# Seven block products from group 2 on, two of them accumulated in PSUM: an attention and feed-forward kernel

## The chip, the cores and the metric

One core of one Trainium2 chip. The metric is the device time of one execution in microseconds; lower is better. Runs shown of the kernel before: 213.74, 213.37 and 212.76, median 213.37.

## The reference

Windowed attention with a linear distance bias and a few global keys, then a feed-forward layer with a softplus.

```
q, k, v: 4 sequences x 8 heads x 768 tokens x 64, float32;  8 global keys, window 96
scores = q k^T / 8 - slope[h] * dist        # dist: |i - j| in the window, 96 at a global key outside it
scores = -1e9 where a key is neither global nor in the causal window of 96
x = softmax(scores) v                       # 3072 tokens x 512
g = softplus(x @ w_in)                      # w_in 512 x 2048
out = g @ w_out                             # w_out 2048 x 512, result float32
```

## The kernel before

**Tiling.** The 3072 tokens are 24 blocks of 128. Two neighbouring blocks of a sequence are a unit (12 units), whose q, k and v are loaded together, 512 KB each. Two blocks are also a group of the feed-forward part (12 groups of 256 tokens). Matmuls are in bfloat16, sums in float32 PSUM.

**Attention of block n.** q and k are cast to bfloat16 (`cast_q`, L622; `cast_rows`, L641), transposed to put the head dimension on partitions (for units 0 to 2 on PE, `transp_pe`; from unit 3 on by a DMA transpose on SP's queue, `transp_dma`, L737), and multiplied for the block itself and the block before it (`scores`, L814). DVE adds the bias (z, L872), ACT takes the exponential (pb, L879), PE multiplies by v with a column of ones (`pv`, L885), DVE normalises (L909, L910), and the result is transposed into XT (`x_transp`, L919: on PE for blocks 0 to 5, by a DMA transpose on SP after that). The keys and values of the first GH rows are copied into the earlier block's buffers for the global keys (`globals_k`, `globals_v`, names gk and gv).

**Feed-forward of group g.** `mm1` (L947) makes the 2048 hidden features in 8 pieces a{g}.{p} of 8 matmuls each (128 x 256 columns), alternating two PSUM banks. ACT takes Exp of each piece (e, L971) and Ln(1 + e) of two pieces together (ln, L982), which gives the softplus g. The second layer has two forms:

- Groups 0 to 2: `mm2` (L996), for each of the two blocks 16 matmuls of 512 columns into one PSUM bank (b{g}.{ns}.{x}), then one copy out (oc, L1032) and a store.
- Groups 3 to 11: seven block products in place of eight (`products`, L456). The group's g is split in four quarters by block (2) and by half of the hidden features (2); w_out is split in four by half of the hidden features and half of the columns. `weight_sums` (L391) forms five sums of w_out's quarters once (ws, 20 operations); `token_sums` (L433) forms five differences of g's quarters for each group (ka, L447). Each product is 8 matmuls of 256 columns, b{g}.3, 4, 5, 2, 1, 7, 6 in this order, and all of groups 3 to 9 go through the one bank o_ps: its lower half takes 3, 5, 7 and 1, its upper half 4, 2 and 6. Groups 10 and 11 spread theirs over several banks (`S_KEYS`). The products are combined in osb, the output buffer, by the operations oe{g}:

| operation | engine | what it does |
|---|---|---|
| a (L498) | ACT or DVE | copies products 3 and 4 to the two off-diagonal quarters |
| b (L477, L478) | DVE | diagonal quarters = off-diagonal ones less 5 and less 2, two operations of 256 columns |
| c (L481) | DVE | off-diagonal quarters + 5 and 2 |
| 1 (L495) | DVE | both diagonal quarters + product 1 |
| 7 (L490) | DVE | diagonal quarters + 7 and 6 (one operation when these lie in one bank, two of L485 when not) |

A product can be written to a half of o_ps only when the operation that reads the earlier product there is done.

**Buffers and loads.** Every load goes to one of 12 raw buffers of 4 KB per partition (NRAW, L307). q, k and v give theirs back; the 8 loads of w_out keep theirs (with 2 spare ones, which hold weight sums), and from the weight sums on three of the 8 return. So 5 rotate later on. The order of the first loads is `FIRST_LOADS` (L152). How far ahead of its block a later unit is loaded is set by `LEADS` (L154) in groups, through a wait on an mm1 piece. Nearly all loads, stores and DMA transposes are issued by SP, whose queue is in order: one that waits holds all behind it.

**Order.** The instruction order of all engines is one written list, `ORDER` (L68): each name with its engine (P PE, V DVE, A ACT, G POOL, S SP). Each engine takes its operations in that order; what an operation waits for follows from the data. 35 filler matmuls (L1116) stand between PE's first operations. The distances for the biases have buffers of their own (rel, far, dist, dist0, L329 to L332).

Of the kernel before, what the change touches and what calls it, by code (L numbers as in the profile page):

```python
# [68 lines left out]
blank:V ldq0.0:A iota:G ldk0.1:S fill0:P ldq0.1:A ldk0.0:S fill1:P dl1a:V fill2:P dl1c:V table:A ldq1.1:S dl0a:V  # L69
fill3:P dl0b:V ldv0:S fill4:P dl0c:V ldk1.0:S dl1e:V fill5:P d0:G fill6:P ldq1.0:S biasTrue6:A d0e:V biasTrue2:A  # L70
fill7:P biasFalse7:V biasFalse0:A biasFalse4:G fill8:P biasFalse3:A ldk1.1:S biasFalse1:A castq0.0:A fill9:P
castk0.1:G ldv1:S biasTrue4:A ident:G biasFalse2:A biasTrue7:A castq0.1:V win1:S biasTrue5:A castk0.0:A biasFalse6:V
trq0.0:P biasTrue1:V biasTrue0:A biasFalse5:V trk0.0:P biasTrue3:V cpq0.0:V fill10:P sb0.0:P cpk0.0:A cpq0.1:V
fill11:P cpk0.1:A castv0.00:G fill12:P fill13:P castq1.1:V ones:G castk1.0:A sc0.0:P sb1.0:P castv0.01:G ex0.0:A
sb1.1:P castq1.0:V ex0.1:A castv0.11:G sc1.0:P sc1.1:P ldq2.0:S ex1.0:A pv0.0:P fill14:P castk1.1:G win0:S nm0.0:V
ex1.1:A ldq2.1:S castv0.10:G trq1.0:P fill15:P ldk2.0:S pv0.1:P cpq1.0:A pv1.1:P nm0.1:V trk1.0:P ldk2.1:S cpq1.1:A
fill16:P nm1.1:V cin1:G pv1.0:P win2:S cpk1.1:A fill17:P xt0:P win3:S nm1.0:V cpk1.0:A fill18:P fill19:P win4:S
castv1.11:G castv1.01:A fill20:P castv1.00:V sc2.0:P win5:S castq2.0:G xt1:P cin0:A win7:S fill21:P z2.0:V fill22:P
fill23:P fill24:P win6:S gv4.1:G z2.1:V sc3.0:P castv1.10:A fill25:P gk4:G wout0:S xc1:V xc0:A fill26:P castq2.1:G
sc3.1:P z3.0:V ex2.0:A a0.1:P castk2.1:G ex2.1:A castk2.0:G pv2.0:P a0.0:P nm2.0:V wout7:S trq2.0:P z3.1:V e0.0:A  # L80
pv2.1:P cin2:G fill27:P ex3.0:A nm2.1:V trk2.0:P ex3.1:A cpq2.0:V fill28:P cin3:G xt2:P fill29:P fill30:P xc2:V
fill31:P e0.1:A fill32:P wout1:S pv3.0:P cin4:G ln0.0:A fill33:P wout2:S a0.3:P nm3.0:V ldv2:S cpk2.0:A a0.2:P
cin5:V e0.3:A cpk2.1:V pv3.1:P wout4:S a0.5:P e0.2:A cpq2.1:V cin7:G wout3:S ln0.1:A a0.4:P nm3.1:V e0.5:A sc4.0:P
cin6:V e0.4:A xt3:P ln0.2:A a0.7:P wout6:S z4.1:V cout0:G a0.6:P e0.7:A xc3:V gv4.0:G z4.0:V fill34:P a1.1:P e0.6:A
ldq3:S wout5:S ex4.1:A cout7:V a1.0:P gk8:V gk5:A cout1:V b0.0.0:P e1.0:A sc5.0:P ws0.6:V e1.1:A b0.0.2:P cout2:G
z5.0:V a1.2:P ln1.0:A a1.3:P ex4.0:A ws0.4:V b0.0.4:P castv2.10:V e1.3:A sc5.1:P castv2.00:V castv2.01:A b1.0.0:P
cout4:G z5.1:V b1.0.2:P e1.2:A pv4.0:P ln1.1:A a1.5:P castv2.11:G nm4.0:V cout3:G b0.1.0:P ln0.3:A ldk3:S pv4.1:P
b0.1.2:P nm4.1:V gv5.0:G gv5.1:A b1.0.4:P e1.5:A a1.4:P ws0.3:V ex5.1:A ws0.1:V b1.0.6:P b0.1.4:P cout6:V castq3.0:A
b0.1.6:P ws1.7:V xt4:P b0.1.8:P ex5.0:A xc4:V a1.7:P ws1.1:V e1.4:A b0.0.6:P ws1.4:V cout5:A ldv4:S pv5.0:P b0.0.8:P
trq3:S nm5.0:V castk3.00:G a1.6:P castk3.01:A ws1.6:V castk3.10:A pv5.1:P castk3.11:A b0.0.10:P nm5.1:V b0.0.12:P  # L90
gk6:A ln1.2:A trk3:S b0.1.10:P ws2.1:V b0.1.12:P ws0.7:V e1.6:A xt5:P b0.1.14:P e1.7:A ws1.3:V ws2.3:G b0.0.14:P
ln1.3:A b1.0.8:P xc5:V ldv3:S ws2.7:V b1.0.10:P castv4.11:A a2.0:P ws2.4:G a2.1:P oc0.0.0:V e2.0:A oc0.1.0:A
b1.0.12:P ws2.6:V e2.1:A b1.0.14:P gv6.0:G ldk4:S sc6.0:P oc1.0.0:A ldq4:S a2.2:P ln2.0:A z6.1:V st0.0.0:S ws3.7:G
ldq5:S a2.3:P e2.2:A z6.0:V ex6.1:A castv3.00:G b1.1.0:P a2.4:P castv3.10:G gk7:A castv3.01:V e2.3:A sc7.0:P e2.4:A
b1.1.2:P ex6.0:A z7.0:V b1.1.4:P castk4.00:G a2.5:P ln2.1:A gv6.1:G castk4.01:V b1.1.6:P castv3.11:G e2.5:A b1.1.8:P
castq4.0:V pv6.0:P ex7.0:A castk4.10:G b1.1.10:P ldk5:S b1.1.12:P nm6.0:V ln2.2:A trq4:S a2.7:P z7.1:V castk4.11:G
b1.1.14:P castv4.00:G pv6.1:P trk4:S a2.6:P oc1.1.0:A nm6.1:V gv7.0:G ex7.1:A b2.0.0:P gv7.1:V xt6:S ws3.3:V e2.7:A
pv7.0:P b2.0.4:P e2.6:A castk5.00:G nm7.0:V ln2.3:A castv4.10:G ldv5:S b2.0.8:P castv4.01:V castk5.10:G gv8.0:A
pv7.1:P b2.0.12:P nm7.1:V ws3.6:G sc8.0:P xt7:S oc2.0.0:A castq5.0:A gv8.1:G z8.1:V b2.1.0:P ws3.4:G st0.1.0:S
castk5.01:A b2.1.4:P trq5:S z8.0:V ex8.1:A b2.1.8:P castk5.11:G gk9:A castv5.10:V castv5.00:G ex8.0:A st1.1.0:S  # L100
sc9.0:P trk5:S a3.0:P castv5.01:G z9.0:V pv8.0:P a3.1:P e3.0:A ldq6:S nm8.0:V st1.0.0:S ex9.0:A z9.1:V pv8.1:P
a3.2:P e3.1:A gv9.0:G ln3.0:A nm8.1:V gv9.1:G ldk6:S ws3.1:G xt8:S pv9.0:P ex9.1:A a3.3:P nm9.0:V gk10:A e3.2:A
pv9.1:P sc10.0:P e3.3:A nm9.1:V a3.4:P castq6.0:G ln3.1:A z10.0:V xt9:S a3.5:P gv10.1:G e3.4:A gv10.0:V ex10.0:A
trq6:S a3.6:P z10.1:V e3.5:A b2.1.12:P castk6.11:G e3.6:A ldq7:S pv10.0:P ex10.1:A ldv6:S castk6.10:G a3.7:P
nm10.0:V ln3.2:A a4.0:P castk6.01:V gk11:G oc2.1.0:V e3.7:A sc11.0:P castk6.00:V ln3.3:A pv10.1:P trk6:S a4.1:P
z11.0:V gv11.1:G gv11.0:A b3.3:P castv5.11:G e4.1:A nm10.1:V st2.0.0:S e4.0:A b3.4:P st2.1.0:S ka3.6:V ldk7:S
ex11.0:A ka3.7:V xt10:S a4.2:P ka3.5:V oe3.a:A a4.3:P castv6.11:G castv6.00:A ka3.2:V ldv7:S e4.2:A ka3.1:G b3.5:P
e4.3:A z11.1:V ln4.0:A pv11.0:P b3.2:P nm11.0:V ex11.1:A a4.4:P oe3.b:V castq7.0:G a4.5:P e4.4:A oe3.c:V pv11.1:P
castv6.01:G sc12.0:P e4.5:A nm11.1:V b3.1:P castk7.00:G ln4.2:A z12.0:V xt11:S a4.6:P z12.1:V ex12.0:A a4.7:P
oe3.1:V ex12.1:A trq7:S castv7.00:G castk7.01:V sc13.0:P e4.7:A castv6.10:G pv12.0:P b3.7:P e4.6:A nm12.0:V ln4.1:A  # L110
castk7.11:G b3.6:P z13.0:V castk7.10:G ln4.3:A a5.1:P castv7.01:G oe3.7:V trk7:S pv12.1:P a5.0:P ka4.7:V e5.1:A
nm12.1:V ex13.0:A b4.3:P ldq8:S ka4.6:V e5.0:A a5.3:P z13.1:V pv13.0:P b4.4:P e5.3:A nm13.0:V ex13.1:A a5.2:P
ka4.5:V oe4.a:A gk14:V a5.5:P ka4.2:V e5.2:A ldk8:S xt12:S pv13.1:P b4.5:P e5.5:A nm13.1:V ln5.0:A b4.2:P ka4.1:V
xt13:S castq8.0:V ln5.1:A a5.4:P oe4.b:V st3.0.0:S sc14.0:P e5.4:A ldv8:S oe4.c:V a5.7:P trq8:S ln5.2:A castk8.01:G
z14.1:V castk8.00:G a5.6:P e5.7:A castv7.11:G z14.0:V b4.1:P ex14.1:A castv7.10:G a6.1:P castk8.10:G gk15:A e5.6:A
oe4.1:V castk8.11:G ex14.0:A sc15.0:P gv14.1:V gv14.0:G trk8:S a6.0:P ln5.3:A z15.0:V b4.7:P e6.1:A ka5.6:G
# [131 lines left out]
def kernel(  # L248
# [440 lines left out]
    def kt_unit(i):  # L689
        return kT_t(i)[:]  # L690
# [581 lines left out]
```

## Time and profile before

The profiled execution:

| | |
|---|---|
| its own time | 213.29 us |
| span from first to last instruction | 211.4 us |
| granted TensorE clock | 1.000 |
| busy us: PE / DVE / ACT / POOL | 202.0 / 161.0 / 179.3 / 106.9 |
| mm1 matmuls (L956) | 768, 94.5 us busy |
| block products (L512) | 504 |
| mm2 matmuls (L1003) | 96 |
| DMA | 40.98 MB, mean 194 GB/s |

Engines: PE is TensorE's matmuls, PEld its weight loads, DVE VectorE, ACT ScalarE, POOL GpSimd, SP SyncE (SPq: the issue of DMAs). Rows of the chain of waits are: start, length, engine and line. Rows of a group are: line, engine, operation, tiles and shapes, count; busy us and mean ns of one; idle time of the engine before them and what ended it. A stretch row is: from and to in us, length, then the busy us of PE, PEld, DVE, ACT and POOL (with counts), granted clock, DMA's busy share, GB/s. Matmul ends are modelled, so the distance between starts tells more of PE than a matmul's own duration. Some matmul records can be missing.

### The profile page before, as it was taken

How to read it: one execution, taken by the hardware profiler on the slowest of the kernel's cores; microseconds unless marked ns; L12 is line 12 of the kernel's file. 1: busy time of each engine (PE TensorE's matmuls, PEld its weight loads, DVE VectorE, ACT ScalarE, POOL GpSimd, SP SyncE). 2: the span in 40 equal slices, each digit the busy share in tenths (PEclk: the TensorE clock that was granted, in tenths of full speed). 3: DMA queues.
4: the chain of work that ended last, by engine and by line, in shares of the span. 5: the costliest groups of instructions: out<-in, count | busy, mean ns of one | idle time of the engine just before them, and what ended most of it. 6: DMA issues, size and time to landing. Idle time of an engine off the chain costs nothing.

```text
span 211.4 us, 5443 instructions
## 1 busy us (share of the span) xinstructions
PE 202.0 (96%) x2176; PEld 161.8 (77%) x2187; DVE 161.0 (76%) x292; ACT 179.3 (85%) x260; POOL 106.9 (51%) x130
## 2 busy tenths in 40 slices
PE   7987999999999988999999999999999999999994
PEld 2564786666765766988988889889889889988883
DVE  4665888888779976988798898786868989624554
ACT  6886999999998899888899989998999899877510
POOL 4466541618769463565038794564465436061070
PEclk9999999999999999999999999999999999999999
DMA  5999999949996899976399988777595510300413
GB/s 202 348 329 321 395 387 353 333 119 211 290 225 154 206 256 177 323 187 126 103 232 185 242 213 175 175 181 174 134 210 130 179 22 3 101 3 0 152 77 122
DMA packets 69848, 40.98 MB, mean 194 GB/s; under 512 B 30144, under 2 KB 61376, under 8 KB 69824
## 3 DMA queue, kind: packets, MB, share of 16 engines
q1 hardware_dynamic: 69392, 39.99, 71.4%
q10 hardware_dynamic: 432, 0.66, 0.9%
q8 instruction: 17, 0.28, 0.6%
q14 instruction: 7, 0.06, 0.1%
HBM read 27.26 MB, written 6.29 MB: 159 GB/s over the span
## 4 chain that ended last, share of the span: by engine, by line
PE 64%; ACT 14%; DMA 11%; SPq 3%; issue 3%; POOL 2%; DVE 2%; DVEq 0%; POOLq 0%
PE h_ps L956 29%; PE o_ps L512 22%; DMA raw<-in_moe_w_out_dram 5%; ACT e L971 4%; PE s_ps L846 4%; DMA raw<-in_moe_w_in_dram 4%; PE x_ps L898 3%; PE o_ps L1003 3%; ACT g L982 3%; ACT pb L879 3%; DMA raw<-in_q_dram 3%; SPq L573 2%; PE x_ps L512 2%; POOL w_out_bf L616 1%; PE s_ps L512 1%
## 5 line engine op out<-in xcount | busy, mean ns | idle before, releaser
L956 PE MATMUL h_ps<-XT,w_in_bf 128*128 128x256 bf16 x768 | 94.5, 273 | 2.4 <-ACT XT L934 1.4
L956 PEld LDWEIGHTS <-w_in_bf 128*128 128x128 bf16 x768 | 72.9, 98 | 13.5 <-issue 1.2
L971 ACT ACTIVATE e<-h_ps 128x512 f32<-128x512 f32 x96 | 58.3, 635 | 11.4 <-PE h_ps L956 11.1
L982 ACT ACTIVATE g<-e 128x1024 bf16<-128x1024 f32 x48 | 49.8, 1056 | 0.8
L872 DVE TENSOR_TENSOR z<-s_ps,biasA 128x1024 f32<-128x1024 f32 x38 | 45.8, 1218 | 4.7 <-PE s_ps L846 2.6
L879 ACT ACTIVATE pb<-z 128x1024 bf16<-128x1024 f32 (+1 forms) x44 | 43.2, 993 | 0.2
L512 PEld LDWEIGHTS <-g 128*128 128x128 bf16 x288 | 27.6, 98 | 3.2
L658 POOL CAST kb<-raw 64x512 bf16<-64x512 f32 x25 | 17.1, 682 | 23.6 <-DMA raw<-in_k_dram 11.0
L447 POOL TENSOR_TENSOR g<-g 128x1024 bf16<-128x1024 bf16 x7 | 15.3, 2187 | 19.3 <-DVE raw L447 17.2
L658 POOL CAST vb<-raw 64x512 bf16<-64x512 f32 x30 | 19.2, 641 | 7.2 <-DMA raw<-in_v_dram 5.8
L512 PEld LDWEIGHTS <-raw 128*128 128x128 bf16 x216 | 20.7, 98 | 2.5
L764 POOL COPY vb<-vb 4x512 bf16<-4x512 bf16 x19 | 12.1, 638 | 19.0 <-PE x_ps L898 18.6
L512 PE MATMUL o_ps<-raw,raw 128*128 128x256 bf16 x168 | 20.8, 273 | 0.0
L898 PEld LDWEIGHTS <-pb 128*128 128x128 bf16 x352 | 16.6, 97 | 4.9 <-ACT pb L879 0.9
L447 DVE TENSOR_TENSOR raw<-g 128x1024 bf16<-128x1024 bf16 x21 | 15.1, 729 | 4.5 <-PE s_ps L512 2.4
L910 DVE TENSOR_TENSOR xs<-x_ps,rcp 128x256 bf16<-128x256 f32 x40 | 17.0, 425 | 1.4
L512 PE MATMUL o_ps<-raw,g 128*128 128x256 bf16 x144 | 18.0, 273 | 0.0
L447 POOL TENSOR_TENSOR raw<-g 128x1024 bf16<-128x1024 bf16 x6 | 13.1, 2184 | 7.8 <-ACT g L982 7.6
L898 PE MATMUL x_ps<-vb,pb 128*128 128x65 bf16 x304 | 15.9, 193 | 0.6 <-DVE xs L910 0.4
L1003 PE MATMUL o_ps<-w_out_bf,g 128*128 128x512 bf16 x59 | 15.4, 379 | 0.4 <-DVE vb L658 0.2
L909 DVE RECIPROCAL rcp<-x_ps 128x4 f32<-128x4 f32 x40 | 7.2, 180 | 10.6 <-PE x_ps L898 10.1
L1003 PEld LDWEIGHTS <-g 128*128 128x128 bf16 x96 | 8.6, 98 | 6.7 <-ACT g L982 0.3
(110 smaller groups left out, 247.4 us busy)
## 6 DMA issues: line engine op xcount, KB each, us to landing
raw<-in_v_dram SPq DMA_DIRECT2D x12, 512.0 KB, 4.8
out_dram<-osb SPq DMA_DIRECT2D x22, 256.0 KB, 2.9
raw<-in_q_dram SPq DMA_DIRECT2D x9, 512.0 KB, 4.3
raw<-in_k_dram SPq DMA_DIRECT2D x9, 512.0 KB, 4.6
raw<-in_moe_w_in_dram SPq DMA_DIRECT2D x8, 512.0 KB, 8.1
raw<-in_moe_w_out_dram SPq DMA_DIRECT2D x8, 512.0 KB, 9.8
raw<-in_k_dram SPq DMA_DIRECT2D x6, 256.0 KB, 5.6
raw<-in_q_dram SPq DMA_DIRECT2D x4, 256.0 KB, 4.9
```

The source lines that it names most:

```text
L447: (nc.vector if eng == "DVE" else nc.gpsimd).tensor_tensor(dst, a[0], b[0], ALU.subtract)
L512: nc.tensor.matmul(psum(j), lhs[:, f // 2, f % 2, :], w(f), start=(f == 0), stop=(f == 7))
L658: copy_on[eng](dst, src)
L764: copy_on[eng](vb_of(prev)[sl, :, 0:D], vb_of(first)[sl, :, 0:D])
L872: nc.vector.tensor_tensor(z, src, bias, ALU.add)
L879: nc.scalar.activation(pb[:, 0:nr, :].rearrange("p (y a) b -> p y (a b)", y=2), src, AF.Exp, scale=1.0 / root_d)
L898: nc.tensor.matmul(xv[:, h, :], pb[:, 4 * (h % 2) + 2 * part + h // 2 if lone else u_all * (2 * (h % 2) + h // 2) + u, :], vb_of(prev if u ...
L910: nc.vector.tensor_tensor(xs[:, 4 * part : 4 * part + 4, :], xv[:, :, 0:D], rcp[:][:, :, None].to_broadcast([P, 4, D]), ALU.mult,)
L956: last = nc.tensor.matmul(hv[:, j, :], w_in_bf[:, m, fb * P : fb * P + P], XT[g % NXG][:, m, :], start=(m == 0), stop=(m == NM - 1),)
L971: nc.scalar.activation(e[:, p % 2, :, :].rearrange("p j (b t r) -> p (j b) r t", b=2, r=2), hb[:].rearrange("p (a r t) -> p a r t", a=4, r=2),
L982: nc.scalar.activation(gt[:, 2 * p - 2 : 2 * p + 2, :].rearrange("p a t -> p (a t)"), e[:].rearrange("p a j t -> p (a j t)"), AF.Ln, bias=1.0,
L1003: nc.tensor.matmul(bank(key)[:, 0 : z - a], gt[:, fb, ns * P : ns * P + P], w_out_bf[:, fb, a:z], start=(fb == 0), stop=(fb == NFB - 1),)
```

## The change

- Group 2 takes the seven products too (`FIRST_S` 3 to 2): ten groups by products, two by `mm2`.
- In groups 2 to 9 (`CHAIN`) the order of products is 3, 4, 1, 5, 2, 7, 6. The operands of 5 and 2 have their sign turned. Products 7 and 6 are accumulated in PSUM on 5 and 2, after operation c has read these. Operation 1 forms the diagonal quarters directly; operation b is gone there. Groups 10 and 11 keep operation b (as an addition) and products 7 and 6 that are not accumulated on others.
- 14 raw buffers. The last holds the distances first and is given to the third load of w_out (`LATE_SLOT`); so 13 are free at the start, and 7 rotate later on. `LEADS` grow by half a group.
- k of units 3 to 11 is cast by one operation of 128 x 1024 in place of four of 64 x 512, and transposed by two DMA transposes of 64 rows (trk{i}.0 and .1) in place of one of 128.
- The written order is another throughout: 1042 names where there were 1061. Among others the loads of k2 and q2 and of w_in are issued in another order, and many casts, copies and sums change engine.

```
-LEADS = {3: 2.25, 4: 2.75, 5: 3, 6: 3, 7: 3.5, 8: 3, 9: 3, 10: 3, 11: 2.75}
+LEADS = {3: 2.75, 4: 3.25, 5: 3.5, 6: 3.5, 7: 4, 8: 3.5, 9: 3.5, 10: 3.5, 11: 3.25}
-FIRST_S = 3
+FIRST_S = 2
+CHAIN = range(FIRST_S, 10)
+LATE_SLOT = ("out", 2)
-    NRAW, NQB, NKB, NQT, NKT, NVB = 12, 2, 2, 3, 3, 6
+    NRAW, NQB, NKB, NQT, NKT, NVB = 14, 2, 2, 3, 3, 6
-    rel = const.tile([P, 2, P], F32, name="rel")
...
+    rel, far, dist = (
+        raw_t[NRAW - 1][:, 256 * x : 256 * x + 256].rearrange("p (a t) -> p a t", a=2) for x in range(3)
+    )
+    dist0 = raw_t[NRAW - 1][:, 768 : 768 + P]
-    idle = deque(range(NRAW))
+    idle = deque(range(NRAW - 1))
+        if name == LATE_SLOT:
+            idle.appendleft(NRAW - 1)
-        for j, a, b in (("6", A21, A11), ("7", A12, A22), ("5", A12, A11), ("2", A21, A22), ("1", A11, A22)):
+        for j, a, b in (("6", A21, A11), ("7", A12, A22), ("5", A11, A12), ("2", A22, A21), ("1", A11, A22)):
-                (dst, keys), after = a, []
+                (dst, keys), after = (b if j in "52" else a), []
-        order = S_ORDER.get(g, "3452176")
+        chain = g in CHAIN
+        order = S_ORDER.get(g, "3415276" if chain else "3452176")
+        def add_m1(eng):
+            nc.vector.tensor_tensor(diag, mid[:, ::-1, :], psum("1")[:, None, :].to_broadcast([P, 2, 256]), ALU.add)
+        def sub_mid(eng):
+            nc.vector.tensor_tensor(mid, mid, bank(s_key(g, "5")).rearrange("p (b c) -> p b c", b=2), ALU.subtract)
-                    nc.tensor.matmul(psum(j), lhs[:, f // 2, f % 2, :], w(f), start=(f == 0), stop=(f == 7))
+                    nc.tensor.matmul(psum(j), lhs[:, f // 2, f % 2, :], w(f), start=(f == 0 and not (chain and j in "267")), stop=(f == 7),
+                                     skip_group_check=chain and j in "5267")
+            if chain:
+                if j == "1":
+                    out_op("1", add_m1, corners + both, "1", at + 1, 0.68)
+                if j in "52" and {"5", "2"} <= have:
+                    out_op("c", sub_mid, both, "5", at + 1, 0.68)
+                if {"6", "7"} <= have:
+                    out_op("7", add_both, corners, "7", at + 1, 0.68)
                 continue
...
+    def cast_k(i, engs, rank):
+        slot = raw_of["k", i]
+        dst = kb[i % NKB][:].rearrange("p a h d -> p (a h d)").rearrange("p (m r y d) -> p m r y d", m=NPAIR, r=2, y=2)
+        src = raw_t[slot][:].rearrange("p (m y r d) -> p m r y d", m=NPAIR, y=2, r=2)
+        op(f"castk{i}.0", engs[0], t_copy(engs[0], 1024, True), rank, lambda eng: copy_on[eng](dst, src),
+           reads=raw_keys(slot), writes=[("kb", i % NKB, x) for x in range(4)], port=True, alts=t_all(1024))
...
+        if which == "k":
+            for x in range(2):
+                dst = kt_unit(i)[:, x].rearrange("p m (r t) -> p (m r) t", r=2)
+                def tr(dst=dst, x=x):
+                    return nc.sync.dma_start_transpose(dst, src[64 * x : 64 * x + 64])
+                op(f"trk{i}.{x}", "SP", 1.3, rank, tr, dma=(0.62, 18.0),
+                   reads=[("kb", i % NKB, y) for y in range(4)], writes=[kt_tile(i) + (x, r) for r in range(2)])
+            return
-            cast_rows(i, "k", e.get("k", ["POOL"]), rank)
+            cast_k(i, e.get("k", ["POOL"]), rank)
```

PE's operations of groups 2 and 3 in the second layer stand in the two orders like this, among the mm1 pieces:

```
before: ... a2.6 b2.0.0 b2.0.4 b2.0.8 b2.0.12 b2.1.0 b2.1.4 b2.1.8 a3.0 ... a3.6 b2.1.12 a3.7 a4.0 a4.1 b3.3 b3.4 ... b3.5 b3.2 ... b3.1 ... b3.7 b3.6
after:  ... b1.1.14 a3.0 a3.1 b2.3 a3.2 b2.4 a3.3 a3.4 a3.5 b2.1 a3.6 a3.7 b2.5 a4.0 a4.1 b2.2 a4.2 b2.7 b2.6 a4.3 a4.4 b3.3 ...
```

More of the change, by code (lines that the diff above doesn't have):

```diff
@@ L474, in products, with first, both_diag, add_m1_late @@
         diag = flat.rearrange("p (a c) -> p a c", c=256)[:, 0:4:3, :]
-        def sub2(eng):
-            nc.vector.tensor_tensor(C[0, 0], C[1, 0], psum("5"), ALU.subtract)
-            nc.vector.tensor_tensor(C[1, 1], C[0, 1], psum("2"), ALU.subtract)
-        def add_mid(eng):
-            nc.vector.tensor_tensor(mid, mid, bank(s_key(g, "5")).rearrange("p (b c) -> p b c", b=2), ALU.add)
+        def first(eng):
+            copy_on[eng](mid, bank(s_key(g, "3")).rearrange("p (b c) -> p b c", b=2))
+        def add_m1(eng):
+            nc.vector.tensor_tensor(diag, mid[:, ::-1, :], psum("1")[:, None, :].to_broadcast([P, 2, 256]), ALU.add)
+        def both_diag(eng):
+            nc.vector.tensor_tensor(C[0, 0], C[1, 0], psum("5"), ALU.add)
+            nc.vector.tensor_tensor(C[1, 1], C[0, 1], psum("2"), ALU.add)
+        def add_m1_late(eng):
+            nc.vector.tensor_tensor(diag, diag, psum("1")[:, None, :].to_broadcast([P, 2, 256]), ALU.add)
+        def sub_mid(eng):
+            nc.vector.tensor_tensor(mid, mid, bank(s_key(g, "5")).rearrange("p (b c) -> p b c", b=2), ALU.subtract)
+        def add_both(eng):
+            nc.vector.tensor_tensor(
+                diag, diag, bank(s_key(g, "7")).rearrange("p (b c) -> p b c", b=2), ALU.add
+            )
         def add_one(j, c):
@@ L487, in add_one @@
             return fn
-        def add_both(eng):
-            nc.vector.tensor_tensor(
-                diag, diag, bank(s_key(g, "7")).rearrange("p (b c) -> p b c", b=2), ALU.add
-            )
-        def add_m1(eng):
-            nc.vector.tensor_tensor(diag, diag, psum("1")[:, None, :].to_broadcast([P, 2, 256]), ALU.add)
-        def first(eng):
-            copy_on[eng](mid, bank(s_key(g, "3")).rearrange("p (b c) -> p b c", b=2))
         def out_op(name, fn, keys, js, at, dur, alts=None):
@@ L586, in fn @@
                 )
-            op(f"ld{which}{i}", "SP", 0.45, rank + 0.01 * z, fn, dma=(1.82, 30.0), sync=sync,
+            op(f"ld{which}{i}", "SP", 0.45, rank + 0.01 * z, fn, dma=(1.86, 30.0), sync=sync,
                writes=raw_keys(slot))
@@ L614, in load_w @@
         op(f"w{which}{p}", "SP", issue, rank, lambda: nc.sync.dma_start(raw, src.rearrange("(a p) c -> p a c", p=P)),
-           writes=raw_keys(slot), dma=cost)
+           writes=raw_keys(slot), dma=cost,
+           after=[u for key in ("rel", ("far", 0), ("far", 1), "dl0", "dl1", "d0") for u in users(key)]
+           if (which, p) == LATE_SLOT else ())
         op(f"c{which}{p}", eng, t_copy(eng, 1024, True), rank, lambda eng: copy_on[eng](dst, raw),
```

192 lines of the change are left out of this document (91 added, 101 removed).

## The prediction

> **What bounds the kernel now.** I first read the page's span and engine shares, then the busy time by stretch, then the chain that ended last in order of time.
>
> ```profile
> span 211.4 us, 5443 instructions
> ...
> PE 202.0 (96%) x2176; PEld 161.8 (77%) x2187; DVE 161.0 (76%) x292; ACT 179.3 (85%) x260; POOL 106.9 (51%) x130
> ```
> ```profile
> 80.00:90.00 10.00, 9.12 (x102) 7.45 (x102) 8.30 (x14) 9.28 (x16) 4.80 (x7) 1.00 1.19 250
> 90.00:100.00 10.00, 10.00 (x125) 8.71 (x123) 8.33 (x17) 8.43 (x12) 6.52 (x9) 1.00 0.71 157
> ```
> ```profile
> 50.97 0.62 ACT vb L658
> ...
> 58.83 0.86 PE o_ps L1003 x4
> ...
> 77.49 1.06 ACT g L982
> 78.55 0.54 ACT e L971
> 79.09 0.93 ACT pb L879
> ...
> 84.02 0.55 PE s_ps L846 x16
> ...
> 85.79 1.75 PE o_ps L512 x16
> ...
> 90.16 0.24 PE x_ps L898 x8
> ...
> 203.91 1.76 PE x_ps L512 x16
> ```
>
> In the two stretch rows the numbers after the length are the busy times of PE, PE's weight loads, DVE, ACT and POOL. From 90 us PE has no idle time at all, and the chain from 85.79 to 203.91 is matmul behind matmul. So there the time is the sum of PE's work and nothing else. Earlier the chain goes through ACT (the rows at 50.97 and from 77.49), which is busy for 9.28 of the ten us from 80. PE is starved a little there: 0.88 us of those ten. After the last matmul come 5.7 us (211.4 less 205.7) of additions, stores and their landing; these don't change. So three sums matter: PE's work, the idle time PE keeps while ACT paces it, and how soon the first real products begin. The other engines matter only where they make PE late.
>
> **The change part by part.**
>
> *Group 2 by seven products.* Removed are 32 matmuls of 512 columns: four take 0.86 us, so 32 take 6.9. Added are 7 x 8 matmuls of 256 columns: sixteen take 1.75, so 56 take 6.1. PE's work falls by **0.8 us**. PE runs this behind the ACT-paced stretch or in it, so I count all of it. It also brings five token sums (three on DVE, two on POOL) and four evictions where two copies were; that work is on engines with room, and is priced with the rivals.
>
> *Two products accumulated on others, groups 2 to 9.* Products 7 and 6 now land on 5 and 2, and the operands of 5 and 2 have their sign turned.
>
> ```profile
> L481 DVE TENSOR_TENSOR osb<-osb,o_ps 128x512 f32<-128x512 f32 x7 | 4.8, 686 | 0.2
> ...
> L477 DVE TENSOR_TENSOR osb<-osb,o_ps 128x256 f32<-128x256 f32 x7 | 2.9, 419 | 3.9 <-PE o_ps L512 3.1 <-ACT e L971 0.7
> L478 DVE TENSOR_TENSOR osb<-osb,o_ps 128x256 f32<-128x256 f32 x7 | 2.9, 413 | 0.0
> ```
>
> In groups 3 to 9 the two operations of L477 and L478 go: 7 x (0.42 + 0.41) = 5.8 us of DVE. None of it is on the path, since PE has no idle time from 90 us on: **0**. What the edit moves is when the bank comes free. Before, three operations (0.42 + 0.41 + 0.69 = 1.5 us) stand between product 2 and product 1. Afterwards one of 0.69 stands between 2 and 7, and one of 0.69 between 1 and 5. The new order puts less PE work there: one mm1 piece and one pv, 0.87 + 0.24 = 1.1 us, in groups 2, 7 and 8. That still covers 0.69, with 0.4 over; if DVE is late, PE waits (a rival).
>
> *k cast in one operation, transposed in two halves.* For units 3 to 11, 36 casts of 64 rows become 9 of 128 rows.
>
> ```profile
> L658 POOL CAST kb<-raw 64x512 bf16<-64x512 f32 x25 | 17.1, 682 | 23.6 <-DMA raw<-in_k_dram 11.0 <-DVE osb L481 10.6 <-issue 1.4
> ...
> L634 POOL CAST qb<-raw 128x1024 bf16<-128x1024 f32 x5 | 5.3, 1051 | 1.9 <-DMA raw<-in_q_dram 1.8
> ```
>
> On POOL that is 1.05 us for a unit where it was up to 4 x 0.68 = 2.7. POOL is busy for half the span, so this alone is worth nothing to the end: **0**. It is spent on casts and sums that the order moves to POOL from ACT and DVE. The price is on SP, in the transposes:
>
> ```profile
> L741 SPq DMA_TRANSPOSE kT<-kb x7: 1232/1232/2062, 47.7 to 160.2; - x7
> ```
> ```profile
> L941 SPq DMA_TRANSPOSE XT<-xs x18: 1188/1217/2171, 63.1 to 181.9; - x18
> ...
> DMA to landing us min/median/max: 2.4/3.3/7.3
> ```
>
> XT's transpose has half of kT's bytes and still holds SP for 1.22 us against 1.23. So a half of k is expected to cost the same as a whole, and SP gets nine more: 9 x 1.22 = 11 us in a queue that issues in order, with all loads, stores and XT transposes behind them. How long a transpose of only 64 rows occupies the DMA engines no row shows. Between a gain (half the rows, so half the time) and a doubling, I take XT's row, which has the same bytes.
>
> The Trainium skill, page "DMA: Bandwidth & Descriptors", section "Rules for kernel authors", speaks against this edit: two transfers to the two halves of the partitions go one behind the other, and one transfer over all 128 is to be used. The two rows above agree with it as far as the issue goes. By the rule the second half is late by a whole transfer, which is the third rival below.
>
> *Fourteen buffers, the distances in the last one, leads longer by half a group.* From the code, the load of q2 waited for the casts of q1, and the w_in loads stood behind it on SP.
>
> ```profile
> 6.21 0.82 SPq L614 DMA_DIRECT2D raw<-in_moe_w_in_dram  x1
> 10.46 0.54 SPq L573 DMA_DIRECT2D raw<-in_q_dram  x1
> ```
> ```profile
> 19.11 1.03 PE L956 MATMUL h_ps<-XT,w_in_bf 128*128 128x256 bf16 x8 [1.38 <-ACT XT L934]
> ...
> 23.02 1.03 PE L1116 MATMUL x_ps<-blank 128*128 128x512 bf16 x4
> ```
>
> SP stands from 7.0 to 10.5. The new order issues w_in 0 to 3 ahead of it, with three quarter-MB loads (q2 twice, half of k2) now behind w_in 2 and 3: 0.79 MB. The DMA rate while these load, from the slices:
>
> ```profile
> GB/s 202 348 329 321 395 387 353 333 119 211 290 225 154 206 256 177 323 187 126 103 232 185 242 213 175 175 181 174 134 210 130 179 22 3 101 3 0 152 77 122
> ```
>
> At about 340 GB/s (its second to fourth values), w_in 2 and 3 land 2.3 us sooner. But w_in 4 to 7 come no sooner, as the bytes ahead of them are the same, and mm1's later pieces need them. The gain is between 0 (the last w_in decides) and 2.3 (all of it passes through). Nearest lies the row of four fillers at 23.02, where PE spends 4 x 0.216 = 0.9 on nothing while it could have run the second pair of mm1 pieces. I take **0.6 us**. The distances in buffer 13 are read out within the first 8 us; the load of w_out 2 that waits for them is issued far later, cost nothing. Longer leads only bring later loads sooner; that removes POOL's waits on k (11.0 us in the row above), which are not on the path.
>
> *The order.* Here I compare ACT's and PE's work between the mm1 pieces of one group and of the next, by the letters of the two orders and the rows above. Worst before is from a3.0 to a4.0: PE 8 x 0.87 + 5 x 0.24 + 0.55 + 0.86 = 9.6 us, ACT 7 x 0.54 + 4 x 0.93 + 3 x 1.06 + 0.2 = 10.9, so PE lacks 1.3. That stretch is where PE's idle time of 80 to 90 us lies. Worst afterwards is from a2.0 to a3.0, because group 2's products move behind it: PE 7 x 0.87 + 3 x 0.55 + 7 x 0.43 + 6 x 0.24 = 12.2 us, ACT 8 x 0.54 + 6 x 0.93 + 3 x 1.06 + 0.62 = 13.7, so PE lacks 1.5. The idle time moves to another place and keeps its size within 0.2 us: **0.**
>
> The sum: -0.8 - 0.6 = **-1.4 us** on the profiled execution. Its own time is 213.29 (211.4 of span and 1.9 around it), against a median of 213.37 of the runs shown. Forecast: **211.9 us**.
>
> **The rivals.**
>
> *The buffers don't bring the first products forward.* PE's first mm1 piece waited on ACT's copy of XT (the 1.38 of the row at 19.11), which hangs on attention, not on w_in alone; and the last w_in is no sooner. Then only the 0.8 stays: 212.5 us.
>
> *The bank is handed over late.*
>
> ```profile
> L872 DVE TENSOR_TENSOR z<-s_ps,biasA 128x1024 f32<-128x1024 f32 x38 | 45.8, 1218 | 4.7 <-PE s_ps L846 2.6
> ```
>
> The cover of 1.1 us holds 0.69 only while DVE is free. If a z of 1.22 is just beginning, 1.22 + 0.69 - 1.1 = 0.8 us of PE is lost. There are three handovers in each of eight groups. Two that hit eat the gain: 213.4 us, no change. For it: DVE is busy for 0.83 of the row 90 to 100. Against it: before, 1.5 us had to fit between products with as little spare, and PE shows no idle time.
>
> *SP becomes the bound (the other side).*
>
> ```profile
> 75.11 3.58 SPq L941 DMA_TRANSPOSE XT<-xs  x2
> ```
> ```profile
> PEld L956 <- DMA XT<-xs: 1.1, 1, 1.1
> ```
>
> Already once PE waited for XT (1.1 us), behind this row, where SP took 3.58 us for two XT transposes that take 2.4 by themselves. For groups 4 and 7 the new order leaves 4.0 us of PE work between the second XT transpose and the first mm1, against a landing of 3.3 us: 0.7 spare. One more transpose of 1.22 in front of it costs 0.5; a trk half waiting for its cast in front costs the wait as well. From one group late in two the gain is gone. If it strikes groups 3 to 7, with 1.0 us each, that is +5.0 - 1.4 = +3.6: 216.9 us; with half of it, 214.4. Against it: the new order places nearly every XT transpose further ahead (3.5 to 6.9 us of PE work for the second block of a group, before 3.1 to 4.9).
>
> *More comes through.* If the 2.3 us of the loads pass to the end and ACT's stretches leave half of their 1.3 us of idle time, it is -0.8 - 2.3 - 0.65 = -3.75: 209.5 us.
>
> **How the numbers follow.** About 0.5% (1.07 us) is what a measurement of this kernel can tell from no change, so faster is below 212.3 and slower above 214.4. Chances: forecast (210.8 to 212.3) 0.45; more comes through 0.10; buffers don't help 0.13; late bank 0.14; SP 0.18. Faster 0.45 + 0.10 = 0.55, same 0.13 + 0.14 = 0.27, slower 0.18. The range reaches from just below 209.5, to let the better case in, up to 215.3, between half of the SP case and the whole: 209.3 to 215.3. About 0.04 lies below and 0.1 above.
>
> **What would show each step.** Right: L512 has 560 matmuls and L1003 64; PE has no idle time from about 85 us to its last matmul; PE's sum falls by 0.8; the first mm1 of L956 begins before 19.11, and its second pair doesn't stand behind four fillers. The bank rival would show as PE waits at L512 on DVE's osb operations. The SP rival would show as PE waits at L956 on XT and SP full between 60 and 100 us. The forecast is wrong if PE's idle time between 20 and 90 us grows by more than 1 us, whatever its releaser.

## The result, and the profile after

| | kernel before | changed kernel | ratio, 95% interval |
|---|---|---|---|
| first comparison, 20 runs each | 213.9 us (212.57 to 215.09) | 212.52 us (211.2 to 213.84) | 0.9934 [0.9911, 0.9956] |
| again (r_after) | 214.09 | 211.88 | 0.9898 [0.986, 0.9936] |
| again (r_after2) | 214.28 | 213.14 | 0.9947 [0.9916, 0.9978] |

Each time here and below is the median of the fast runs: some executions take over 1.5% longer than the fastest of the same kernel, most of them at a lower granted clock, and are left out.

The change makes the kernel faster by 1.4 us in the first comparison (0.9 to 1.9 by the interval), by 2.2 and 1.1 in the two others. The forecast was -1.4 us. The experiments show that two terms of the sum were wrong all the same, and a third, the 0.6 of the loads, isn't found in the profiles.

The page of the changed kernel, its span and engine shares:

```profile
span 210.6 us, 5494 instructions
...
PE 201.3 (96%) x2211; PEld 164.4 (78%) x2211; DVE 156.1 (74%) x287; ACT 174.6 (83%) x248; POOL 105.5 (50%) x113
```

PE's sum fell by 0.7 us, DVE's by 4.9, ACT's by 4.7 and POOL's by 1.4, and the span by 0.8. Most of what came off the three other engines is not seen in the span.

PE's busy time in four stretches, of before and then of the changed kernel (the number after the length is PE's):

```profile
20.00:30.00 10.00, 9.58 (x122) 7.96 (x121) 8.00 (x16) 8.96 (x13) 5.79 (x7) 1.00 1.05 393
30.00:60.00 30.00, 29.53 (x272) 20.15 (x276) 25.28 (x42) 29.10 (x44) 15.32 (x18) 1.00 0.93 264
60.00:90.00 30.00, 28.26 (x308) 20.72 (x310) 25.40 (x41) 27.17 (x40) 17.44 (x24) 1.00 0.99 226
90.00:200.00 110.00, 110.00 (x1256) 96.75 (x1254) 84.47 (x151) 97.98 (x136) 53.09 (x58) 1.00 0.59 140
```
```profile
20.00:30.00 10.00, 8.98 (x112) 7.33 (x111) 7.89 (x17) 8.32 (x12) 6.21 (x9) 1.00 1.07 374
30.00:60.00 30.00, 29.97 (x299) 20.16 (x297) 26.43 (x44) 28.99 (x40) 21.15 (x26) 1.00 1.10 283
60.00:90.00 30.00, 28.59 (x343) 24.49 (x342) 23.93 (x43) 27.79 (x40) 16.14 (x19) 1.00 1.13 235
90.00:200.00 110.00, 109.89 (x1238) 96.63 (x1236) 75.25 (x134) 94.71 (x134) 50.25 (x39) 1.00 0.59 130
```

From 20 to 90 us PE is idle for 2.63 us before and 2.46 after. The idle time moved and kept its size. From 90 us on PE is full in both.

The two largest of PE's waits from 17 us on, of before and then of the changed kernel (us in total, times, longest):

```profile
PE h_ps L956 <- ACT XT L934: 1.4, 1, 1.4
...
PE h_ps L956 <- ACT g L982: 0.8, 1, 0.8
```
```profile
PE s_ps L875 <- DMA kT<-kb: 1.3, 1, 1.3
PE h_ps L985 <- POOL w_in_bf L627: 1.3, 2, 0.7
```

The waits on ACT's XT and on ACT's g are replaced by a wait on one half of a k transpose, and by two on GpSimd's casts of w_in. The chain of the changed kernel shows the first: the half was issued at 72.18 behind two 512 KB loads and took 6.81 us to land.

```profile
72.18 6.81 DMA kT<-kb
```

PE's rows at the start, of the changed kernel and then of before:

```profile
18.69 1.05 PE L985 MATMUL h_ps<-XT,w_in_bf 128*128 128x256 bf16 x8 [0.53 <-POOL w_in_bf L627]
...
21.68 1.05 PE L985 MATMUL h_ps<-XT,w_in_bf 128*128 128x256 bf16 x8 [0.73 <-POOL w_in_bf L627]
...
28.39 0.23 PE L875 MATMUL s_ps<-qT,kT 64*128 64x128 bf16 x2
```
```profile
24.34 1.91 PE L956 MATMUL h_ps<-XT,w_in_bf 128*128 128x256 bf16 x16
...
28.22 0.23 PE L846 MATMUL s_ps<-qT,kT 64*128 64x128 bf16 x2
```

The first mm1 piece begins 0.42 us earlier (19.11 before) and the third 2.66 us earlier (24.34 before). Yet at the same score block, with 48 mm1 matmuls done in both, the changed kernel is at 28.39 and the old one at 28.22. The same 66 operations of PE stand ahead of this block in both orders, the fillers among them, so up to there PE has stood idle about as long. Its very first filler, for one, waits 2.2 us in the changed kernel where it waited 1.2. The early start was spent before 28 us.

### The profile page after: what moved, and what is told of

Read it like the earlier page. It is cut to its first block, busy times and chain, and to the rows that moved or that the text cites. A ratio compares the mean times of both kernels' runs of the same rounds, so it can differ in the third digit from the quotient of the medians.

```text
span 210.6 us, 5494 instructions
## 1 busy us (share of the span) xinstructions
PE 201.3 (96%) x2211; PEld 164.4 (78%) x2211; DVE 156.1 (74%) x287; ACT 174.6 (83%) x248; POOL 105.5 (50%) x113
## 3 DMA queue, kind: packets, MB, share of 16 engines
q1 hardware_dynamic: 69680, 39.99, 76.2%
## 4 chain that ended last, share of the span: by engine, by line
PE 68%; DMA 13%; POOL 5%; ACT 5%; DVE 4%; issue 2%; ACTq 0%; SPq 0%; POOLq 0%; DVEq 0%
PE h_ps L985 31%; PE o_ps L519 20%; DMA raw<-in_k_dram 5%; PE s_ps L875 4%; PE x_ps L927 4%; PE s_ps L1032 3%; DMA kT<-kb 3%; DMA raw<-in_q_dram 3%; DMA qT<-qb 2%; PE o_ps L1032 2%; POOL raw L449 2%; ACT pb L908 2%; ACT e L1000 2%; ACT g L1011 1%; POOL g L449 1%
## 5 line engine op out<-in xcount | busy, mean ns | idle before, releaser
L519 PEld LDWEIGHTS <-g 128*128 128x128 bf16 x320 | 30.8, 98 | 3.6
L449 POOL TENSOR_TENSOR raw<-g 128x1024 bf16<-128x1024 bf16 x11 | 23.5, 2142 | 19.3 <-ACT g L1011 12.8
L449 POOL TENSOR_TENSOR g<-g 128x1024 bf16<-128x1024 bf16 x9 | 19.5, 2171 | 12.3 <-DVE raw L449 9.7
L793 POOL COPY vb<-vb 4x512 bf16<-4x512 bf16 x16 | 9.8, 612 | 31.7 <-PE x_ps L927 30.6
L519 PEld LDWEIGHTS <-raw 128*128 128x128 bf16 x240 | 23.1, 98 | 2.9
L519 PE MATMUL o_ps<-raw,raw 128*128 128x256 bf16 x192 | 24.1, 273 | 0.0
L519 PE MATMUL o_ps<-raw,g 128*128 128x256 bf16 x160 | 20.1, 273 | 0.0
L519 PE MATMUL o_ps<-w_out_bf,g 128*128 128x256 bf16 x128 | 16.1, 272 | 0.0
L1145 PE MATMUL x_ps<-blank 128*128 128x512 bf16 x35 | 12.2, 436 | 2.2 <-DVE blank L1084 2.2
L483 DVE TENSOR_TENSOR osb<-osb,o_ps 128x512 f32<-128x512 f32 x8 | 5.5, 686 | 10.3 <-PE o_ps L519 8.1
```

What stands on the lines that cost most here:

```text
L449: (nc.vector if eng == "DVE" else nc.gpsimd).tensor_tensor(dst, a[0], b[0], ALU.subtract)
L519: nc.tensor.matmul(psum(j), lhs[:, f // 2, f % 2, :], w(f), start=(f == 0 and not (chain and j in "267")), stop=(f == 7), skip_group_check ...
L1145: nc.tensor.matmul(x_ps[:], blank[:, 0:P], blank[:])
```

## The experiments

Each time is from one comparison, beside the kernel before on the same chip. Unless another is named, an experiment is an edit of the changed kernel. What an edit costs over the changed kernel is taken between the two ratios, with 0.9934 for the changed kernel (0.001 is 0.21 us). By its ratios of the two other comparisons every such cost would be 0.8 us more or 0.3 less. In lines of the order, names that stand between those shown are left out. Where lines are named, the edits shift line numbers by up to fifteen, and those in a fence are that kernel's own.

**The changed kernel again** (r_after, r_after2).

> The changed kernel as it is, to set the others against on one chip. Its median was 1.4 us below that of the kernel before (212.5 against 213.9), and that should return: a ratio of 0.993 to 0.994.

> The changed kernel again, as the mark for the three beside it: both theories expect a ratio to the kernel before of about 0.992 (0.9934 and 0.9898 in its first two comparisons), and PE waits of about 1.3 us on the k transpose near 79 us.

The ratios are in the first table: 0.9898 and 0.9947, one below and one above what was expected, and a gain each time. PE waited 1.4 and 0.8 us on kT, so this wait is in all three profiles of the changed kernel; its size varies, and so does the span (211.3 and 210.7).

**Group 2 back on mm2** (e_g2).

```
-FIRST_S = 2
+FIRST_S = 3
-b2.3 b2.4 b2.1 b2.5 b2.2 b2.7 b2.6
+b2.0.0 b2.0.4 b2.0.8 b2.0.12 b2.1.0 b2.1.4 b2.1.8 b2.1.12
```

> The changed kernel with group 2 back on 32 matmuls of 512 columns, at the places where its products stood; its token sums and additions go, two copies come. Theory (group 2's products are worth PE's 0.8 us and nothing hides it): 0.8 us more than the changed kernel, about 213.3 us, ratio near 0.997, with the wait at 79 us still there. Rival (the gain is that of the buffers, the loads and the order): within 0.3 us of the changed kernel.

213.62 us, ratio 0.9972 [0.9935, 1.0008], which is 0.8 us over the changed kernel (0.5 to 1.6 by that kernel's three ratios). That is what the theory expected of the matmuls. The interval overlaps two of the changed kernel's three and touches the third, so 0.8 is a size and not a proof. The wait on the k transpose is still there, as expected (3.0 us). The rest of this profile isn't read, since the granted clock was 0.83 from 80 to 90 us.

**The k edit undone** (e_kwhole).

```
-castk10.0:V ... trk10.0:S ... trk10.1:S
+castk10.00:V castk10.01:V castk10.10:V castk10.11:V ... trk10:S
```

> The changed kernel with k of units 3 to 11 as before: four casts of 64 rows and one transpose of 128, in the changed order, with the transpose where the first half stood. Theory (two halves cost SP and the DMA engines about twice one whole, and this is what made k late at 79 us; the casts lie beside other work): the share of the load queue falls from 76.2% to about 71.4%, the wait at 79 us goes, and the time falls by 0.5 to 1.3 us to 211.2 to 212. Rival (the casts are what the k edit is for, and 27 casts more make DVE and POOL late): 0.5 to 2 us more than the changed kernel.

215.78 us, ratio 1.007 [1.004, 1.01]: 2.9 us over the changed kernel, and slower than before. The wait on the k transpose is gone, as the theory expected, but the time rises by more than even the rival's 2 us. My price of nothing falls. (For units 3 and 11, two of the four casts also stand on another engine than the one cast did.) PE's waits and then DVE's and GpSimd's rows around the largest:

```profile
PE x_ps L927 <- DVE xs L939: 2.2, 2, 1.9
...
PE h_ps L985 <- DMA XT<-xs: 1.7, 1, 1.7
```
```profile
133.29 3.55 DVE L677 CAST kb<-raw 64x512 bf16<-64x512 f32 x4
136.85 0.69 DVE L901 TENSOR_TENSOR z<-s_ps,bias 128x512 f32<-128x512 f32 x1
```
```profile
134.37 2.18 POOL L449 TENSOR_TENSOR raw<-g 128x1024 bf16<-128x1024 bf16 x1 [1.46 <-PE o_ps L519]
```
```profile
134.14 0.42 DVE kb L677
...
134.58 2.26 DVE kb L677
```

Four casts stand on DVE's queue ahead of z, and PE waits at the end of that row of work. Three take 0.42 us or less. The last starts just after GpSimd's subtraction, takes 2.26 us, and ends 0.29 us after it (136.84 against 136.55). The changed kernel has one cast in this place, of 0.67:

```profile
130.69 0.67 DVE L657 CAST kb<-raw 128x1024 bf16<-128x1024 f32 x1
```

The Trainium skill, page "SBUF — State Buffer", section "Who interferes with whom", says that DVE and GpSimd share a port pair, that a DVE cast can need it, and that the second to issue is blocked until the first ends. These rows agree.

That place is not the whole loss. In this profile PE is 2.6 us behind the changed kernel already at the score block ahead of it (131.97 against 129.38), and 4.4 us at its last products (210.80 against 206.37).

**Four casts, half transposes kept** (e_k4).

```
-copy_on[eng](dst, src)
+copy_on[eng](dst[rows, half], src[rows, half])
-castk10.0:V
+castk10.00:V castk10.01:V castk10.10:V castk10.11:V
```

> The changed kernel with each later k tile cast in four operations of 64 partitions by 512 columns, on the engines that cast it whole (one of unit 3's on DVE, one on GpSimd); the two half transposes stay. Theory of the casts: what was lost with the k edit undone (2.9 us) comes from the 27 added casts, on DVE above all, so that most of it shows here too, about 2 us over the changed kernel, with waits of PE for work of DVE (xs, qb) of about 2 us. Theory of the transposes: what was lost comes from the single large transpose, whose halves now land apart; then this kernel is within 0.5 us of the changed one. The theory of the prediction, casts at nothing, also expects within 0.5 us.

213.69 us, ratio 0.9978 [0.994, 1.0016]: 0.9 us over the changed kernel, with intervals that overlap. After its first filler PE waits on DVE nowhere. The same four casts aren't held up by GpSimd's subtraction:

```profile
131.62 1.52 DVE L664 CAST kb<-raw 64x512 bf16<-64x512 f32 x4
```
```profile
132.70 2.43 POOL L451 TENSOR_TENSOR raw<-g 128x1024 bf16<-128x1024 bf16 x1 [1.46 <-PE o_ps L521]
```

Three of them begin before the subtraction. The fourth begins 0.02 us after it (132.72), and takes 0.42 us all the same; the subtraction takes 2.43 us where the last one took 2.18. So neither theory is met. The added casts alone cost about half of the 2 us I expected, or less, and the rest of the 2.9 comes with the whole transposes or with where the casts fall.

**The same, with four casts moved behind z** (e_kwhole2, an edit of e_kwhole).

```
-castk10.00:V castk10.01:V castk10.10:V castk10.11:V ... z18.0:V ... nm17.0:V
+z18.0:V ... nm17.0:V castk10.00:V castk10.01:V castk10.10:V castk10.11:V
```

> The changed kernel with the k edit undone, as before, and unit 10's four k casts moved on DVE's queue from ahead of the score operation of group 18 to behind it and the normalisation that follows. In the profile of the first form one of these four casts took 2.26 us beside a GpSimd subtraction (the others 0.42), and PE waited 1.9 us for the xs behind them. Theory: that place is most of what the first form lost, so the PE wait on xs goes and the time falls by 1 to 2 us, to within 0.5% of the kernel before. Rival: the loss sits in the k work as a whole (the single transposes, XT late) and comes out at another place: within 0.5 us of the first form, 0.7% over the kernel before.

214.38 us, ratio 1.0008 [0.9979, 1.0038]: a fall of 1.3 us, in the size that the theory asked for (from 1.007). But its profile shows the same collision, with another victim:

```profile
133.16 1.49 DVE kb L677
```
```profile
133.08 3.76 DVE L677 CAST kb<-raw 64x512 bf16<-64x512 f32 x4
136.85 0.69 DVE L496 TENSOR_TENSOR osb<-osb,o_ps 128x512 f32<-128x512 f32 x1
```
```profile
PE o_ps L519 <- DVE osb L496: 1.6, 1, 1.6
```

The first cast begins during GpSimd's subtraction (132.39 to 134.52) and ends 0.13 us after it. The casts now hold up the read-out of a product bank, and PE waits 1.6 us for that where it waited 1.9 for xs. The profiles lay most of the fall elsewhere. This is the score block ahead of the casts, which e_kwhole reaches at 131.97:

```profile
129.99 0.40 PE L875 MATMUL s_ps<-qT,kTa 64*128 64x128 bf16 x8
```

Of the 2.3 us between the two spans (214.9 and 212.6), 2.0 are there before the edit does anything. So the fall can't be laid to the move, and what made it stays open.

**The k edit alone, on the kernel before** (b_kcast).

```
-castk10.01:G castk10.00:G castk10.11:V castk10.10:G ... trk10:S
+castk10.0:G ... trk10.0:S trk10.1:S
```

> The kernel before with the k edit alone: each later k tile cast in one operation (GpSimd, for unit 3 ACT) and transposed in two halves, both where the one transpose stood. In the changed order the edit undone cost 2.9 us. Theory of the prediction, the edit by itself at nothing: within 0.5 us of the kernel before. Theory of the edit's own worth: 2 us or more under the kernel before. Rival, SP: nine more issues of 1.2 us stand ahead of XT's transposes and the stores in an order that was not written for them, 1 us or more slower, with PE waits on XT or on k's transpose.

215.6 us against 214.31, ratio 1.0069 [1.0037, 1.0102]: the edit that is worth 2.9 us in one order costs about 1.4 in the other. The rival is right. PE's waits, and SP's queue (start, length):

```profile
PE h_ps L971 <- DMA XT<-xs: 2.4, 2, 1.8
```
```profile
74.23 2.54 SPq L749 DMA_TRANSPOSE kT<-kb  x2
...
78.62 3.43 SPq L956 DMA_TRANSPOSE XT<-xs  x2
```
```profile
80.83 5.46 DMA XT<-xs
```

A pair of halves holds SP for 2.54 us, where one whole transpose of before held it for 1.23 (72.00 to 73.23). The two XT behind it start at 78.62, before at 75.11; this pair makes 1.3 of that delay. The second XT then takes 5.46 us to land, about as long as before (5.35), and PE stands. The profiled pair differs by 3.8 us, more than the medians. Of that 1.7 us are there by 20 us, ahead of the first cast that the edit touches, with a granted clock of 0.82 from 10 to 16 us; most of the rest comes at these two waits.

**The old order of the first loads** (e_loads). w_in 0, 2 and 3 go back behind the loads of k2 and q2 that they stood behind; k2 stays ahead of q2, and the 14 buffers stay.

```
-... win0 ldk1.1 ... ldk2.0 win3 ... win2 ldk2.1 ldq2.0 ldq2.1 win5 ...
+... ldk1.1 ... ldk2.0 win0 ... ldk2.1 ldq2.0 ldq2.1 win2 win3 win5 ...
```

> The changed kernel with the loads of the first weight pieces in the order of before: piece 0 behind k2's first half, pieces 2 and 3 behind the last half of q2. Theory of the prediction: the first products of mm1 come 0.4 us later and the second pair up to 2.6 us later, behind fillers, of which 0.4 to 0.6 us reach the end. Rival: the starved stretch between 20 and 90 us takes it up and the time is within 0.3 us of the changed kernel.

215.5 us, ratio 1.0067 [1.0034, 1.01]: 2.8 us over the changed kernel (2.4 by the medians of the comparison that they share). Both expectations were too small. PE's third mm1 piece, and ACT ahead of it:

```profile
23.60 1.03 PE L984 MATMUL h_ps<-XT,w_in_bf 128*128 128x256 bf16 x8 [2.11 <-ACT e L999]
```
```profile
21.98 1.04 ACT L626 CAST w_in_bf<-raw 128x1024 bf16<-128x1024 f32 x1 [2.17 <-DMA raw<-in_moe_w_in_dram]
22.93 1.14 ACT L999 ACTIVATE e<-h_ps 128x512 f32<-128x512 f32 x2
```

The late load holds ACT in the cast that the changed order gave it. The Exp of the first pieces stands behind that cast, and PE needs the banks which Exp reads. At the score block that the changed kernel reaches at 28.39 this one is 1.5 us late, and it is still 1.5 us late at 100 us:

```profile
29.89 0.23 PE L874 MATMUL s_ps<-qT,kT 64*128 64x128 bf16 x2
...
105.48 0.40 PE L926 MATMUL x_ps<-vb,pb 128*128 128x65 bf16 x8 [0.94 <-DVE xs L938]
```

Another 1.6 us are lost between 102 and 113 us, where PE waits 0.94 us for xs and 0.3 for XT; no row ties these to the first loads. So 1.5 us is what the early loads are seen to be worth to the changed order. In the kernel before, GpSimd had that cast and PE ran fillers, so they are not worth as much against it.

**No accumulation** (e_nochain).

```
-CHAIN = range(FIRST_S, 10)
+CHAIN = ()
-b5.1 oe5.1 b5.5 b5.2 oe5.c b5.7 b5.6 oe5.7
+b5.5 b5.2 oe5.b oe5.c b5.1 oe5.1 b5.7 b5.6 oe5.7
```

> The changed kernel with the products of groups 2 to 9 each in a bank of their own, in the order 3452176 and with the DVE operation that adds two of them (0.73 us each) back, eight in all and so 5.8 us of DVE. Theory of the prediction: DVE has the room, so within 0.4 us of the changed kernel. Rival: DVE is crowded now that it casts k for four units, so that half of the 5.8 us or more reaches PE: 1.5 us or more over the changed kernel, with waits of PE on DVE's work of that size.

225.58 us, ratio 1.0532 [1.0488, 1.0577], 12.8 us over the changed kernel. Ahead of the run I wrote that each product would have a bank of its own; that is not so, and all still go through o_ps. PE's waits, and the first of these places on DVE:

```profile
PE o_ps L518 <- DVE osb L492: 8.4, 7, 1.6
PE o_ps L518 <- POOL g L448: 2.2, 2, 1.5
```
```profile
96.11 0.42 DVE L485 TENSOR_TENSOR osb<-osb,o_ps 128x256 f32<-128x256 f32 x1 [0.70 <-PE o_ps L518]
96.45 0.41 DVE L486 TENSOR_TENSOR osb<-osb,o_ps 128x256 f32<-128x256 f32 x1
96.89 0.69 DVE L492 TENSOR_TENSOR osb<-osb,o_ps 128x512 f32<-128x512 f32 x1
```

The two operations of b and the one of c stand between product 2 and product 1, 96.11 to 97.58, and the new order has one mm1 piece there. PE waits in seven groups, 1.2 us each. The 2.2 us on GpSimd are for differences of g, which the old order of products needs earlier. This does not tell what DVE's added work costs; it tells what it costs inside a bank handover that has no cover. The PE work laid around the products was not moved back, so 12.8 us isn't what the accumulation gains over the kernel before, which had more cover there.

**DVE's room by itself** (e_dve).

```
+AGAIN = {2: "7", 3: "1", 4: "7", 5: "6", 6: "1", 7: "6", 8: "7"}
+            if AGAIN.get(g) == j:
+                op(f"ka{g}.{j}x", "DVE", 0.0, rank, ex, ...)
```

> The changed kernel with seven subtractions of g (one for each of groups 2 to 8) done twice in a row on DVE, the second writing the same values: 7 x 0.68 = 4.8 us of DVE added, with no PSUM bank held longer. It measures DVE's room apart from the banks, which the kernel with one bank for each product could not. Theory of the prediction: DVE has the room, within 0.4 us of the changed kernel (about 213.1 in its last two comparisons). Rival: DVE is crowded, 1.5 us or more over it.

213.92 us, ratio 0.9987 [0.9961, 1.0014], 1.1 us over the changed kernel, which was not run beside it; the interval lies above two of the changed kernel's three and overlaps the third. Between the two: DVE's room is not free. Its page, and then DVE's rows and PE's at the longest of the waits:

```profile
PE 202.9 (96%) x2211; PEld 165.1 (78%) x2211; DVE 161.6 (76%) x294; ACT 174.7 (83%) x248; POOL 105.9 (50%) x113
```
```profile
166.80 1.78 DVE L449 TENSOR_TENSOR raw<-g 128x1024 bf16<-128x1024 bf16 x2
168.50 0.68 DVE L482 COPY osb<-o_ps 128x512 f32<-128x512 f32 x1
```
```profile
169.24 1.03 PE L521 MATMUL o_ps<-raw,raw 128*128 128x256 bf16 x8 [0.63 <-DVE osb L482]
```

The doubled subtraction stands ahead of the copy out of the bank, and PE waits for that copy. DVE is busy 5.5 us longer than in the first profile (156.1), and about a fifth of that reaches the end, though DVE is idle for a quarter of the span.

**The k half ahead of loads and stores, and ahead of loads alone** (e_trk5, e_trk5b).

```
e_trk5:   trk5.0 trk5.1 st1.1.0 xt8 st0.0.0 ldv6 ldk6
e_trk5b:  trk5.0 st1.1.0 xt8 st0.0.0 trk5.1 ldv6 ldk6
changed:  trk5.0 st1.1.0 xt8 st0.0.0 ldv6 ldk6 trk5.1
```

> The changed kernel with one SP operation moved: the second half of unit 5's k transpose stands right behind the first, ahead of the store, the XT transpose and the two loads of 0.5 MB that stood between. Theory (after 20 us the time is PE's work and the few places where PE stands): PE's wait of 1.30 us at 79 us goes and nothing takes its place, so 1.0 to 1.3 us less than the changed kernel, about 211.3 us, ratio 0.987 to 0.989. Rival (the slack is given back: the XT transpose and the loads behind it are late in turn, and PE stands later): within 0.3 us of the changed kernel.

> The changed kernel with the second half of unit 5's k transpose ahead of the two loads it stands behind, but still behind the two stores that it had been moved past in the earlier try. Theory: the PE wait of 0.8 to 1.3 us on the k transpose near 79 us goes or halves, and the stores land when they did, so that ACT does not wait for an output buffer; 0.5 to 1 us under the changed kernel. Rival: PE's slack is given back at the next late thing (the loads, now 1.2 us later on SP), within 0.3 us of the changed kernel or slower.

213.79 us (ratio 0.9975 [0.994, 1.001]) and 214.04 us (0.9969 [0.9931, 1.0007]): 0.9 and 0.7 us over the changed kernel, where the theory expected 0.5 to 1.3 under it. In both the wait on kT is gone, and in both another took its place, here from e_trk5's PE, ACT and chain:

```profile
PE o_ps L518 <- ACT osb L479: 2.7, 1, 2.7
```
```profile
ACT osb L479 <- DMA out_dram<-osb: 3.5, 1, 3.5
```
```profile
71.60 4.19 DMA out_dram<-osb
```

The store that frees an output buffer lands 4.19 us after its issue (e_trk5b: 4.27); in the changed kernel it is issued at 70.36 and lands 2.5 us later. ACT's copy into that buffer waits for it, and PE waits for the copy. Moving a transpose that holds SP for 1.2 us forward took away a wait of 1.3 and gave one of 2.7 (2.2) elsewhere. The rival had the mechanism right both times; in size the first try is slower than the 0.3 us that it allowed.

## Why the prediction was right, and where it was not

- **What bounds the kernel.** Right. From 90 us PE stays full in both kernels (109.89 of 110 in the changed one). One reading was off: the last products of PE start at 207.24 before and 206.37 after, not near 204; the chain leaves PE for DVE at 205.75 before, and at 200.47 in the changed kernel. From PE's last start to the end it is 4.2 us in both, and the sum did not use the tail.
- **Group 2, -0.8.** Right. The changed profile has 64 mm2 matmuls and 560 block products; PE's last products start 0.87 us earlier; undone, the edit costs about 0.8.
- **Accumulation, 0.** The bank handovers are right: in the changed kernel PE waits for none of DVE's osb operations. That DVE's 5.8 us cost nothing is wrong: 4.8 us added cost about 1.1, and the longest wait stands in a region where PE "has no idle time". A full PE shows that DVE was just in time, not that it had room.
- **k, 0.** This is the step that failed, in both directions. The halves do hold SP as long as a whole (2.54 for two), as I took it from XT's row, and alone they cost 1.4 us by the third rival's mechanism. In the changed order the edit is worth 2.9. There DVE casts k for four units, at 0.67 to 1.0 us in place of 1.5 to 3.6 for four casts, ahead of z, xs and the bank read-outs. The casts make about 0.9 of the 2.9 (e_k4); how the other 2.0 comes about is not shown. I priced the casts by GpSimd's row and by its share, but the order puts them on DVE. On the rule cited from the Trainium skill, page "DMA: Bandwidth & Descriptors", section "Rules for kernel authors", the two orders differ: with halves the old one is slower (b_kcast, which changes the casts too), the changed one faster (e_k4 against e_kwhole, four casts in both).
- **Loads, -0.6.** The signs came as listed (18.69 before 19.11; no row of four fillers). The gain isn't in the profiles: at 28 us both kernels stand level. The traces show w_in 3 landing at 18.17 where it landed at 21.83, but w_in 2 as before (20.53 and 20.50) and the last w_in 0.7 later (27.99 and 27.25). That is the lower end of my range, where "the last w_in decides". Undone in the changed order it costs 2.8, of which 1.5 are seen at its own place, since ACT now casts that piece.
- **Order, 0.** Right in size (2.63 and 2.46 us of idle time), but I named a wrong place and cause: the wait at 79 us comes behind a3.0, and it is for the k half and not for ACT's arithmetic.

Why did the sum come out? In part by luck. The terms do not add. Undone one at a time in the changed order, three parts cost 0.8, 2.9 and 2.8 us, 6.5 together, against a gain of 1.4; and one of them is a loss of 1.4 in the old order. It looks as if each order fits the durations it was written for: every single edit tried here, in either direction, cost something by its median. The profiled pair differs by 0.8 us and the medians by 1.4; no row was found for the 0.6 between, and repeated spans of one kernel differ by as much (210.6, 211.3, 210.7). So the -0.8 of group 2 is seen in the profiled pair, and the rest is not assigned. The sum was made for the profiled execution, and there only its first term came. That is the rival in which the buffers don't bring the first products forward: it gave 212.5 us, and 212.52 was measured. The forecast of the time, 211.9, was 0.6 lower; the difference of 1.4 came out because the kernel before has a median of 213.9 in twenty runs, and not the 213.37 of three that I started from.

## What to carry to other kernels

In a kernel with a written order, price an edit together with the order that comes with it: find on which engine the operation stands afterwards and what is queued behind it there. A part undone alone measures how far the order depends on it, not what it brought. And a wait at a crowded queue that is taken away by moving one transfer forward can come back one transfer later, and larger, as it did in both tries here.

## What the hardware showed that I had not expected

A DVE cast of 0.42 us took 2.26 when it began 0.2 us after a GpSimd subtraction (e_kwhole), and 0.42 when it began 0.02 us after one (e_k4). The share of the 16 DMA engines rose at equal bytes, from 71.4% to 76.2% of the span, and I first laid that to the half transposes. The rows of e_kwhole and of b_kcast:

```profile
q1 hardware_dynamic: 69392, 39.99, 74.0%
```
```profile
q1 hardware_dynamic: 69680, 39.99, 74.4%
```

The first has whole transposes in the changed order: 74.0% of 214.9 is 159.0 us, against 160.5 in the changed kernel, 156.7 in e_k4 with halves (74.0% of 211.8), and 150.9 before. So in the changed order the halves do not make it. In the old order it comes with them: 74.4% of 215.2 is 160.1 us in b_kcast. What makes it isn't settled; three profiles of the changed kernel itself lie between 160.5 and 165.0.
